# Where the first sets of w1 sums are loaded, and when a tile's results and the w2 sums are made, in a Strassen FFN fused with attention

## The chip, the core and the metric

The kernel runs on one core of one Trainium2 chip. The metric is the time of one execution on the device in microseconds (us), lower is better. Three runs of the kernel before took 535.15, 537.13 and 540.07 us; the median is 537.13 us. A change of about 1% (5.4 us) is what a measurement of this kernel can tell from no change.

## What is computed

```python
scores = scale * np.matmul(q, k.transpose(0, 1, 3, 2))      # q, k, v: 8 x 12 x 448 x 64
x = np.matmul(np.maximum(scores, 0.0) ** 2 / S, v)          # then as tokens: 8 x 448 x 768
mu = np.mean(x, axis=-1, keepdims=True)
var = np.mean((x - mu) ** 2, axis=-1, keepdims=True)
xn = (x - mu) / np.sqrt(var + 1e-06) * g_ln
out = x + np.maximum(xn @ w_ch1, 0.0) @ w_ch2               # w_ch1: 768 x 3072, w_ch2: 3072 x 768
```

There is no softmax: the scores are cut at zero and squared. The 1/sqrt(var) of the layer norm is applied after the second product, as a factor of each token, and g_ln and the mean are folded into w1.

## The kernel before, in words

The eight batches are worked on in four pairs (0 to 3) of 896 tokens. Each pair goes through attention, a first FFN product (xn @ w_ch1, then a relu on ScalarE) and a second one. TensorE's work is interleaved by hand: `interleave` (L13) hands out the attention of pair p+1 in bundles of three score tiles between the units of the second FFN product of pair p. Every engine runs its instructions in program order, so an instruction that waits holds up all that stand behind it on its engine. A bundle is 12 matmuls `sc_ps` (L364), three relus on ScalarE (L375), and squares, two on VectorE (L379) and, for pairs 1 and 3, one on ScalarE (L377).

From pair 1 on, the first FFN product is a Strassen product (`ffn1_pair`, L763). w1 and x are cut in 2 x 2 blocks, and seven products of sums of blocks take the place of eight. Its function `run` (L921) goes through 12 steps (n = 0 to 11); a step has seven products of three matmuls of 448 columns, in the order 3, 4, 1, then 7 and 6 of the step before (`close`, L862), then 5 and 2. Beside them ScalarE copies the first result to `z` (L928) and does the relus (L857), and VectorE does four additions (L930, L932, L944, L947). Products 5 and 2 cannot start before the copy (L928) and the first addition (L930) of their step. Products 1, 2, 5, 6 and 7 take sums of blocks of x (`x_sum`, made at the stage's start by `start`, L880, and by `even` and `odd`, L869 and L876).

The five sums of blocks of w1 that a step needs, a *set*, are computed once, in pair 1's first FFN product, and written to a DRAM tile `kept`. Pairs 2 and 3 load them again (`given`): `sums_early(n)` (L804) loads what products 3, 4 and 1 read, on SyncE's queue for sets 0 to 2 and on ScalarE's for the others; `sums_late(n)` (L820) loads what products 6 and 7 read, on SyncE's queue. There is room for three sets at a time. Set 0 lies in `room0`. For pair 2, sets 1 and 2 lie in four buffers of the pool `attn`, which holds the squared scores (`w_sum` in the profile). For pair 3, the last, all pools of the attention (`heads`, L78) are closed first, and a new pool `late` in their place (`prepare`, L1167) holds the sets (`w_room`) and five sums of x.

SyncE's queue carries, in program order, the writes of the results (`out_dram`, L756, two for each half tile), these loads, the transposing DMAs of k and q for the attention (L311, L316, L317), and the DMAs that transpose x to tokens (`xtok_sb`, L637). For pair 3 these last are 24: six at the hook `odd` (L1195), and three, three, six and six in the steps 0 to 3 (`between_three`, L1187). Eight DMA semaphores are handed out in turn to the DMAs of the two queues, SyncE's and ScalarE's, and a DMA is not issued before the previous one on its semaphore has landed. In the program, ScalarE's load of set 7, which stands between the relus of step 4 and the copy L928 of step 5, shares its semaphore with the first of the six transposes that belong to step 3.

`between_two` (L1171) puts the sums of blocks of w2, which the Strassen form of the second FFN product of pairs 2 and 3 reads, into pair 2's first FFN product: t3 and t4 as 24 subtractions on GpSimd (L988), two a step, and t7 as three additions on VectorE (L985), one in each of the steps 1 to 3. t1 and t6 are made earlier, by six additions on VectorE beside pair 1's second FFN product (L1249), and take two quarters of w1 that no step reads any more; t7 lies in `spare`.

The second FFN product of pairs 2 and 3 is `strassen_units` (L1197). A token tile has 128 tokens, and a pair seven tiles: the odd one, tile 3, is done directly in `ffn2_mid` (L1013), and the other six, as three pairs of tiles, by seven products each (`ffn2_pair`, L1048). `ffn2_mid` accumulates in two PSUM banks, one for each half of the columns; `finish` (L741) computes the result of a half on VectorE (L745), which frees the bank, and stores it. The sums of h that the first pair of tiles needs are made by `h_sums_of` (L999): s1 (L1007), s2 and s5 (L1005), s6 (L1009), s7 (L1011). The first product of `ffn2_pair` takes the first of these two banks for pair 2; for pair 3 it takes other banks.

A few lines that the change touches (L1035 to L1046):

```python
        nc.vector.tensor_add(s[:, n], h[:, 0, n], h[:, 1, n])
        for name in ("s1", "s2", "s6", "s7"):
            h_sums_of(pair, 0, (name,))
        yield from most(a, s, "t2")
        yield
        yield from most(b, s, "t5")
        yield
        ...
        for half, ps in enumerate((a, b)):
            finish(pair, 3, half, 0, K1, ps, (nc.sync, nc.sync))
```

Of the kernel before, what the change touches and what calls it, by code (L numbers as in the profile page):

```python
# [28 lines left out]
def kernel(  # L29
# [733 lines left out]
    def ffn1_pair(pair, keep=False, given=False, prepare=None, between=None):  # L763
# [8 lines left out]
        w, temps, rooms = {}, [], [None] * 3  # L772
        kinds = {3: (0, 3), 4: (3, 6), 1: (6, 9), 6: (9, 12), 7: (12, 15), "16": (6, 12)}

        def room_of(t, late=None):

            if t is None:
                return {}
            r = {m: t[:, a:b] for m, (a, b) in kinds.items() if b <= t.shape[1]}
            if late is not None:  # L780
                r.update({m: late[:, a - 9:b - 9] for m, (a, b) in kinds.items() if a >= 9})
            r["early"] = [(t[:, :9], 0)]
            r["late"] = [(t[:, 9:] if late is None else late, 9)]
            return r
        rooms[0] = room_of(room0)
# [5 lines left out]
        wide_x = prepare is not None  # L791

        def x_sum(m, a, b, op):
            if wide_x:
                op(x[m], a, b)
            else:
                op(x[m][0], a[:, :2], b[:, :2])
                op(x[m][3], a[:, 2], b[:, 2])
# [5 lines left out]
        def sums_early(n):  # L804
# [4 lines left out]
            w[n].update(rooms[n % 3])  # L809
# [10 lines left out]
        def sums_late(n):  # L820
            if n >= KH:
                return
            if given:
                w[n].update(rooms[n % 3])
                fetch(nc.sync, n, "late")
                return
# [42 lines left out]
        def even():  # L869
            sums_early(0)  # L870
            if not wide_x:
                nc.vector.tensor_add(x[5], lo[:, :KQ], lo[:, KQ:])
                sums_late(0)
                sums_last(0)

        def odd():  # L876
            if not wide_x:
                nc.vector.tensor_sub(x[6], hi[:, :KQ], lo[:, :KQ])

        def start():  # L880
            z = x_room[:, 0].rearrange("p c s -> p (c s)")
            temps.extend(z[:, i * S2:(i + 1) * S2].bitcast(fp32) for i in range(2))
            if wide_x:
                pool = prepare()
                for i in range(3):
                    t = pool.tile([P, 6 if i == 0 else 15, P], bf16, tag=f"w1_{i}", name=f"w1_room{i}")
                    rooms[i] = room_of(room0[:, :9], t) if i == 0 else room_of(t)
                xs = pool.tile([P, 5, KQ, S], bf16, tag="x_sum", name="x_sum")
                x.update({m: xs[:, i] for i, m in enumerate((1, 2, 7, 5, 6))})
                sums_late(0)  # L890
            else:
                hold_x = [apool.tile([P, 2, 512], bf16, tag="attn", name="x_sum")[:, :, :S] for _ in range(5)]
                for m, t, rest in ((1, 0, (3, 0)), (2, 1, (3, 1)), (7, 2, (4, 0))):
                    x[m] = (hold_x[t], hold_x[t][:, 0], hold_x[t][:, 1], hold_x[rest[0]][:, rest[1]])
                for i in range(1, 3):
                    one, two = (apool.tile([P, 2, 512], bf16, tag="attn", name="w1_sum")
                                .rearrange("p r (c n) -> p (r c) n", n=P) for _ in range(2))
                    if given:
                        rooms[i] = {3: one[:, :3], 4: one[:, 3:6], 1: (None, one[:, 6], one[:, 7], two[:, 0]),
                                    6: two[:, 1:4], 7: two[:, 4:7],  # L900
                                    "early": [(one, 0)], "late": [(two[:, :7], 8)]}
                    else:
                        rooms[i] = {3: two[:, :3], "4a": one[:, 6:8], "4b": two[:, 6],
                                    4: (None, one[:, 6], one[:, 7], two[:, 6]),
                                    1: one[:, :3], 6: one[:, 3:6], 7: two[:, 3:6], "16": one[:, :6]}
            if given:
                for n in (1, 2):
                    sums_early(n)
                    sums_late(n)
            x_sum(1, lo[:, :KQ], hi[:, KQ:], nc.vector.tensor_add)  # L910
            if wide_x:
                x_sum(5, lo[:, :KQ], lo[:, KQ:], nc.vector.tensor_add)
            x_sum(2, hi[:, :KQ], hi[:, KQ:], nc.vector.tensor_add)
            x_sum(7, lo[:, KQ:], hi[:, KQ:], nc.vector.tensor_sub)
            if wide_x:
                x_sum(6, hi[:, :KQ], lo[:, :KQ], nc.vector.tensor_sub)
# [56 lines left out]
    def w2_sum_units(name):  # L973
# [5 lines left out]
        def four(c):  # L979
            if name == "t7":  # L980
                to = w2_sum[name][:, 4 * c:4 * c + 4]
            else:
                at = w1[:, c, KH * P:] if name == "t1" else w1[:, KQ + c, :KH * P]
                to = at.rearrange("p (k n) -> p k n", n=DH)
            nc.vector.tensor_add(to, x[:, 4 * c:4 * c + 4], y[:, 4 * c:4 * c + 4])  # L985

        def one(k):
            nc.gpsimd.tensor_sub(w2_sum[name][:, k], x[:, k], y[:, k])  # L988
        if name in ("t3", "t4"):
# [23 lines left out]
    def ffn2_mid(pair, a, b):  # L1013
# [22 lines left out]
        for name in ("s1", "s2", "s6", "s7"):  # L1036
            h_sums_of(pair, 0, (name,))
        yield from most(a, s, "t2")
        yield
        yield from most(b, s, "t5")  # L1040
        yield
        for half, ps, left, name, then in ((0, a, h[:, 1], "t4", "t2"), (1, b, h[:, 0], "t3", "t5")):
            rows(ps, left, name, n, KH)
            rows(ps, s, then, n, KH, last=True)
        for half, ps in enumerate((a, b)):
            finish(pair, 3, half, 0, K1, ps, (nc.sync, nc.sync))  # L1046

# [119 lines left out]
    def prepare():  # L1167
# [145 lines left out]
```

## Time and profile before

The profiled execution took 538.45 us, of which its span, from the first to the last instruction, is 536.5 us; the median of the three runs is 1.32 us under it.

| what | value |
|---|---|
| span of the profiled execution | 536.5 us |
| TensorE busy | 514.6 us, 96% of the span |
| VectorE busy | 384.0 us, 72% |
| ScalarE busy | 308.9 us, 58% |
| GpSimd busy | 109.7 us, 20% |
| mean granted TensorE clock | 0.986 |
| pair 2's first FFN product, 297 to 354 us | TensorE busy 53.61 us of 57 |
| its second one, beside pair 3's attention, 354 to 425 us | 66.94 us of 71 |
| pair 3's first FFN product, 425 to 491 us | 59.26 us of 66 |
| its second one, 491 to 536.5 us | 41.26 us of 45.5 |

How to read it: in a row of instructions, *engine line operation out<-in* is followed by the count; in the timeline the first two columns are the start and the duration in us, and a bracket tells the idle time of the engine before the row and what ended it. "SPq" and "ACTq" are DMA issues on the queues of SyncE and ScalarE. A list of waits gives the sum in us, the count and the longest. A row of a window gives busy time of each engine, the granted clock as a share of the full one, the share of time in which the DMA engines were busy, and GB/s.

### The profile page before, as it was taken

To read this page: it belongs to the slowest core of one execution; us is meant where nothing else is said; L and a number is where in the kernel's file an instruction comes from. 1 tells how busy PE (TensorE), PEld (TensorE's weight loads), DVE (VectorE), ACT (ScalarE), POOL (GpSimd) and SP (SyncE) were. 2 spreads that over 40 slices of the span, in tenths; PEclk is the share of its full clock that TensorE was granted. 3 is DMA by queue.
4 is the path that set the end of the run, shared out by engine and by line. 5 is a ranking of instruction groups with operands and counts; after the bars stand their busy time and mean duration, and the time that the engine had idled before them with its cause. 6 is when DMAs were issued, how large, how long until landed. Compare 5 with 4: busy or idle time off the path is not lost.

```text
span 536.5 us, 11444 instructions
## 1 busy us (share of the span) xinstructions
PE 514.6 (96%) x4565; PEld 302.4 (56%) x4565; DVE 384.0 (72%) x723; ACT 308.9 (58%) x495; POOL 109.7 (20%) x150
## 2 busy tenths in 40 slices
PE   8999999999999999999999899989999977999996
PEld 6687779755555545555555445544555434455663
DVE  5875754598998998768876598765876836776653
ACT  6966775588584567566463366766878244571000
POOL 7334102112212475002102592001200000000000
PEclk9999999999999999999999899998999989899999
DMA  9999999999899856249959954107983284511222
GB/s 197 206 205 208 211 190 160 149 182 184 150 189 177 171 171 172 67 89 154 156 131 167 224 145 130 55 1 135 165 133 77 51 221 108 152 51 28 62 59 59
DMA packets 125478, 74.34 MB, mean 139 GB/s; under 512 B 80882, under 2 KB 121842, under 8 KB 125426
## 3 DMA queue, kind: packets, MB, share of 16 engines
q1 hardware_dynamic: 94994, 42.17, 39.6%
q0 software_dynamic: 26976, 25.50, 31.4%
q10 hardware_dynamic: 3456, 5.97, 3.9%
q8 instruction: 35, 0.57, 0.5%
q14 instruction: 17, 0.14, 0.1%
HBM read 63.70 MB, written 16.91 MB: 150 GB/s over the span
## 4 chain that ended last, share of the span: by engine, by line
PE 88%; DVE 3%; ACT 3%; DMA 2%; SPq 2%; issue 2%; ACTq 0%
PE m_ps L853 26%; PE o_ps L734 19%; PE m_ps L1064 8%; PE h_ps L675 7%; PE o_ps L1064 7%; PE sc_ps L364 7%; PE av_ps L396 6%; PE o_ps L1023 2%; PE h_ps L719 2%; PE h_ps L701 2%; ACT early L375 1%; DMA w_sum<-kept 1%; ACT attn_sb L375 1%; PE tr_ps L249 1%; PE idle_ps L235 1%
## 5 line engine op out<-in xcount | busy, mean ns | idle before, releaser
L375 ACT ACTIVATE attn_sb<-sc_ps 128x896 bf16<-128x896 f32 (+4 forms) x150 | 126.2, 902 | 51.6 <-PE sc_ps L364 43.7
L734 PE MATMUL o_ps<-w,hT_sb 128*128 128x384 bf16 x672 | 116.0, 326 | 0.0
L857 ACT ACTIVATE hT_sb<-m_ps 128x448 bf16<-128x448 f32 x144 | 78.1, 544 | 56.3 <-PE m_ps L853 53.7
L734 PEld LDWEIGHTS <-hT_sb 128*128 128x128 bf16 x672 | 63.0, 98 | 48.8 <-issue 10.1
L379 DVE TENSOR_TENSOR attn_sb<-attn_sb 128x896 bf16<-128x896 bf16 x98 | 59.8, 621 | 32.8 <-ACT attn_sb L375 32.2
L675 PE MATMUL h_ps<-x_room,w 128*128 128x256 bf16 (+2 forms) x384 | 43.8, 263 | 0.3 <-ACT early L375 0.3
L928 ACT COPY x_room<-m_ps 128x448 f32<-128x448 f32 x36 | 19.1, 532 | 37.0 <-PE m_ps L853 31.4
L1064 PEld LDWEIGHTS <-hT_sb 128*128 128x128 bf16 x288 | 27.8, 98 | 20.1 <-issue 2.5
L944 DVE TENSOR_TENSOR m_ps<-x_room,m_ps 128x448 f32<-128x448 f32 x36 | 22.6, 628 | 22.9 <-ACT hT_sb L857 22.5
L675 PEld LDWEIGHTS <-w 128*128 128x128 bf16 x384 | 33.8, 97 | 7.0 <-issue 2.6
L853 PE MATMUL m_ps<-x_sum,w 128*128 128x448 bf16 x144 | 33.3, 352 | 4.4 <-ACT x_room L928 2.8
L853 PEld LDWEIGHTS <-w_sum 128*128 128x128 bf16 x240 | 23.4, 98 | 24.6 <-DMA w_sum<-kept 2.4
L853 PEld LDWEIGHTS <-w 128*128 128x128 bf16 x216 | 21.1, 98 | 25.2 <-issue 5.7
L402 DVE TENSOR_SCALAR xT_sb<-av_ps 128x896 bf16<-128x896 f32 (+2 forms) x30 | 27.0, 900 | 10.6 <-PE av_ps L396 10.4
L158 POOL DMA_DIRECT2D k_sb<-in_k_dram x15 | 10.7, 712 | 107.6 <-DMA kT_sb<-k_sb 83.9
L1064 PEld LDWEIGHTS <-x_room 128*128 128x128 bf16 x216 | 20.9, 99 | 19.3 <-issue 6.4
L158 POOL DMA_DIRECT2D v_sb<-in_v_dram x20 | 14.2, 711 | 83.1 <-PE sc_ps L364 74.5
L364 PE MATMUL sc_ps<-qT_sb,kT_sb 64*64 64x448 bf16 x392 | 28.5, 364 | 1.2 <-ACT hT_sb L857 0.6
L930 DVE TENSOR_TENSOR x_room<-x_room,m_ps 128x448 f32<-128x448 f32 x36 | 21.6, 600 | 10.0 <-ACT x_room L928 5.9
L652 DVE BATCH_NORM_STATS2 stats<-xtok_sb 128x6 f32<-128x384 bf16 x56 | 28.3, 547 | 0.1
L685 ACT ACTIVATE hT_sb<-h_ps 128x256 bf16<-128x256 f32 (+1 forms) x49 | 18.0, 368 | 16.0 <-PE h_ps L675 15.1
L377 ACT ACTIVATE attn_sb<-attn_sb 128x896 bf16<-128x896 bf16 x28 | 26.6, 950 | 0.9
(170 smaller groups left out, 846.8 us busy)
## 6 DMA issues: line engine op xcount, KB each, us to landing
out_dram<-o_room SPq DMA_DIRECT2D x108, 96.0 KB, 2.2
w<-in_moe_w_ch_dram POOLq DMA_DIRECT2D x12, 384.0 KB, 14.2
w<-in_moe_w_ch_dram POOLq DMA_DIRECT2D x4, 1152.0 KB, 20.5
q_sb<-in_q_dram POOLq DMA_DIRECT2D x20, 224.0 KB, 5.9
v_sb<-in_v_dram POOLq DMA_DIRECT2D x20, 224.0 KB, 6.0
k_sb<-in_k_dram POOLq DMA_DIRECT2D x15, 224.0 KB, 5.9
w_room<-kept SPq DMA_DIRECT2D x12, 192.0 KB, 2.7
kept<-room SPq DMA_DIRECT2D x4, 480.0 KB, 2.8
```

The costliest lines, as they stand in the source:

```text
L364: nc.tensor.matmul(ps[cols, r, o * w:(o + 1) * w], g["k"](i)[rows, cols], g["q"](i, r)[rows, blk[0]:sum(blk), cols], start=True, stop=True)
L375: nc.scalar.activation(a, ps[:, :, :len(slots) * w], ACTF.Relu)
L377: nc.scalar.activation(a, a, ACTF.Square)
L379: nc.vector.tensor_mul(a, a, a)
L396: nc.tensor.matmul(ps[cols, hh, :w], v_sb[rows, pr, j * D:(j + 1) * D], g["attn"][i][rows, r, :], start=(j == 0), stop=(j == J - 1))
L402: nc.vector.tensor_scalar_mul(x, ps[:, :, :w], score_scale)
L652: nc.vector.bn_stats(stats[:, n], xtok[pair][:, n * G:(n + 1) * G, t, :])
L675: nc.tensor.matmul(ps[:, :w + more], w1[:, c, ni * P:(ni + 1) * P], xc[b][:, c, s.start:s.stop + more], start=(c == 0), stop=(c == K1 - 1))
L734: nc.tensor.matmul(ps[:, :DH], hT[pair][:, ki, t * P:(t + 1) * P], w2[:, ki, cols], start=(o == 0), stop=(o == K2 - 1))
L853: nc.tensor.matmul(ps, *at, start=(first and c == 0), stop=(c == KQ - 1), skip_group_check=not first)
L857: nc.scalar.activation(hT[pair][:, n + KH * row, half * S:(half + 1) * S], ps, ACTF.Relu)
L1064: nc.tensor.matmul(ps, x[:, ki], y[ki] if isinstance(y, list) else y[:, ki], start=(first and ki == 0), stop=(ki == KH - 1), skip_group_ch ...
```

## The change

- **Pair 2's sets 1 and 2** are loaded at the hook `even`, behind set 0, into the quarter of w1 that t1 took until then, instead of into `w_sum` at the stage's start. Set 4 and later go to the `attn` buffers as before.
- **Pair 3's sets.** The pools of the attention are no longer closed, and there is no pool `late`. The rest of set 0 and the sets 1 and 2 are loaded at the hook `odd`, ahead of the six token transposes, into the buffers of q and k, whose last transposes are done. The sums x5 and x6 are made at `odd` too, in the two buffers of transposed q; the other three x sums take `attn` buffers in six additions, as in pairs 1 and 2.
- **`ffn2_mid`** finishes the first half tile before it starts the second one's last products, and puts each half's result ahead of the sums of h: s1, result, s2 with s5, result, s6, s7. It is one unit shorter, three units in place of four are kept for after the attention, and no bundle is placed ahead of the units.
- **w2 sums.** t1 moves from VectorE, beside pair 1's second FFN product, to GpSimd in pair 2's first one: 12 additions behind the 24 subtractions, three a step. t7 moves from the steps 1 to 3 of that stage to VectorE beside pair 1's second FFN product. t6 stays there at other units.

The matmuls are the same in number and shape. The diff, cut to its core:

```diff
-    def ffn1_pair(pair, keep=False, given=False, prepare=None, between=None):
+    def ffn1_pair(pair, keep=False, given=False, late=False, between=None):
...
+        def room_of_two(one, two):
+            return {3: one[:, :3], 4: one[:, 3:6], 1: (None, one[:, 6], one[:, 7], two[:, 0]),
+                    6: two[:, 1:4], 7: two[:, 4:7], "early": [(one, 0)], "late": [(two, 8)]}
...
+        rooms[0] = room_of(room0, room0[:, 9:])
+        if late:
+            rooms[0] = room_of(room0[:, :9], chunks(slots["k"][1], 6))
+            rooms[1] = room_of_two(chunks(qbuf[0], 8), chunks(qbuf[1], 7))
+            rooms[2] = room_of_two(chunks(qbuf[2], 8), chunks(slots["k"][0], 7))
+            for m, t in ((5, slots["qT"][1]), (6, slots["qT"][0])):
+                x[m] = t.rearrange("p a b -> p (a b)")[:, :KQ * S].rearrange("p (c s) -> p c s", s=S)
+        elif given:
+            quarter = [chunks(w1[:, c, KH * P:], KH) for c in range(KQ)]
+            for n in (1, 2):
+                once[n] = room_of(quarter[n - 1][:, :9], quarter[2][:, 6 * (n - 1):6 * n])
...
-            w[n].update(rooms[n % 3])
+            w[n].update(once.get(n) or rooms[n % 3])
...
         def even():
             sums_early(0)
-            if not wide_x:
+            if not late:
                 nc.vector.tensor_add(x[5], lo[:, :KQ], lo[:, KQ:])
                 sums_late(0)
                 sums_last(0)
+                if given:
+                    for n in (1, 2):
+                        sums_early(n)
+                        sums_late(n)
 
         def odd():
-            if not wide_x:
-                nc.vector.tensor_sub(x[6], hi[:, :KQ], lo[:, :KQ])
+            if late:
+                nc.vector.tensor_add(x[5], lo[:, :KQ], lo[:, KQ:])
+                for n in range(3):
+                    if n:
+                        sums_early(n)
+                    sums_late(n)
+            nc.vector.tensor_sub(x[6], hi[:, :KQ], lo[:, :KQ])
...
-            if given:
-                for n in (1, 2):
-                    sums_early(n)
-                    sums_late(n)
...
         def one(k):
-            nc.gpsimd.tensor_sub(w2_sum[name][:, k], x[:, k], y[:, k])
-        if name in ("t3", "t4"):
+            if name == "t1":
+                nc.gpsimd.tensor_add(w2_sum[name][k], x[:, k], y[:, k])
+            else:
+                nc.gpsimd.tensor_sub(w2_sum[name][:, k], x[:, k], y[:, k])
+        if name in ("t3", "t4", "t1"):
...
-        for name in ("s1", "s2", "s6", "s7"):
-            h_sums_of(pair, 0, (name,))
-        yield from most(a, s, "t2")
-        yield
-        yield from most(b, s, "t5")
-        yield
+        h_sums_of(pair, 0, ("s1",))
         for half, ps, left, name, then in ((0, a, h[:, 1], "t4", "t2"), (1, b, h[:, 0], "t3", "t5")):
+            if half:
+                yield
+            yield from most(ps, s, then)
             rows(ps, left, name, n, KH)
             rows(ps, s, then, n, KH, last=True)
-        for half, ps in enumerate((a, b)):
             finish(pair, 3, half, 0, K1, ps, (nc.sync, nc.sync))
+            for more in (("s2",), ("s6", "s7"))[half]:
+                h_sums_of(pair, 0, (more,))
...
-            side.update(gps=w2_sum_units("t3") + w2_sum_units("t4"), t7=w2_sum_units("t7"),
+            side.update(gps=w2_sum_units("t3") + w2_sum_units("t4") + w2_sum_units("t1"),
                         tokens=token_units(2, range(NT)))
...
-        if 0 < n <= KQ:
-            side["t7"].pop(0)()
-        for _ in range(2):
+        for _ in range(3):
             side["gps"].pop(0)()
...
-            sums = w2_sum_units("t1") + w2_sum_units("t6")
-            units = beside_of(units, {8 + 6 * n: f for n, f in enumerate(sums)})
+            sums = w2_sum_units("t6") + w2_sum_units("t7")
+            units = beside_of(units, dict(zip((12, 20, 28, 43, 45, 47), sums)))
...
-        few = 4 if last else 3
-        interleave(units[:-few], beside, 0, 1 if last else 0)
+        few = 3
+        interleave(units[:-few], beside)
         for f in left:
             f()
         wide.close()
-        if last:
-            heads.close()
         hook("start")
```

## The prediction

> **What bounds the kernel now.** The page gives TensorE 96% of the span, so only its idle time and its slow clock can be gained; no work on it is added or removed. I read the list of TensorE's waits first, because it tells how long it stood still and for whom.
>
> ```profile
> PE m_ps L853 <- DMA w_room<-kept: 3.5, 1, 3.5
> PE o_ps L1064 <- DVE o_room L745: 3.2, 1, 3.2
> PE m_ps L853 <- ACT x_room L928: 2.8, 1, 2.8
> PE m_ps L853 <- DMA w_sum<-kept: 2.0, 1, 2.0
> PE m_ps L853 <- DVE x_room L930: 1.6, 2, 1.1
> ```
>
> These five are 13.1 us. By the timeline they lie, in order: A, 300.11 to 302.08, pair 2's step 1 waits for set 1, which SyncE issued only at 295.76; B, 319.28 to 320.43, step 4 waits for VectorE; C, 360.25 to 363.41, the first product of `ffn2_pair`; D, 428.62 to 432.11, pair 3's step 1 waits for set 1 (with 0.47 for VectorE just ahead of it); E, 452.70 to 455.48, pair 3's step 5 waits for ScalarE's copy L928.
>
> Second, windows behind these places, for the granted clock (busy times of PE, PEld, DVE, ACT and POOL, then the clock, the DMA share and GB/s).
>
> ```profile
> 300.00:305.00 5.00, 3.03 (x12) 1.36 (x12) 2.21 (x5) 1.20 (x3) 3.52 (x5) 0.81 1.16 314
> 305.00:310.00 5.00, 5.00 (x23) 2.37 (x22) 2.33 (x4) 2.71 (x5) 5.00 (x7) 0.84 1.21 141
> 364.00:368.00 4.00, 4.00 (x24) 1.57 (x22) 1.42 (x3) 2.92 (x4) 0.00 (x0) 0.57 0.66 143
> 432.00:436.00 4.00, 3.89 (x13) 1.72 (x14) 1.24 (x2) 0.53 (x1) 0.00 (x0) 0.61 0.97 284
> 456.00:482.00 26.00, 26.00 (x130) 12.97 (x128) 20.40 (x42) 16.72 (x33) 0.00 (x0) 0.93 0.36 105
> ```
>
> A, C, D and E are each followed by lost clock: 5 x 0.19 + 5 x 0.16 = 1.75 us, 4 x 0.43 = 1.72, 4 x 0.39 = 1.56, 26 x 0.07 = 1.82. I take 1.7 us for each: a stall that goes takes this with it. B, of 1.15 us, has no such stretch behind it.
>
> Third, the timelines of C and E, and SyncE's queue ahead of E.
>
> ```profile
> 357.28 0.95 DVE L1007 TENSOR_TENSOR x_room<-hT_sb 128x1536 bf16<-128x1536 bf16 x1
> 358.15 1.75 DVE L1005 TENSOR_TENSOR x_room<-hT_sb 128x3072 bf16<-128x3072 bf16 x1
> 359.93 0.96 DVE L1009 TENSOR_TENSOR hT_sb<-hT_sb 128x1536 bf16<-128x1536 bf16 x1
> 360.81 0.95 DVE L1011 TENSOR_TENSOR hT_sb<-hT_sb 128x1536 bf16<-128x1536 bf16 x1
> 362.75 1.13 DVE L745 SCALAR_TENSOR_TENSOR o_room<-o_ps,rstd_sb,xtok_sb 128x384 f32<-128x384 f32 x2
> 363.41 0.81 PE L1064 MATMUL o_ps<-w,x_room 128*128 128x384 bf16 x4 [3.15 <-DVE o_room L745]
> ```
>
> At C the matmuls of the odd tile are done at 360.25; its result, which frees the bank, stands on VectorE behind all the sums of h and two squares.
>
> ```profile
> 418.43 1.11 SPq L756 DMA_DIRECT2D out_dram<-o_room  x2
> 419.58 7.70 SPq L637 DMA_TRANSPOSE xtok_sb<-xT_sb  x6
> 427.39 1.17 SPq L756 DMA_DIRECT2D out_dram<-o_room  x2
> 428.79 2.31 SPq L789 DMA_DIRECT2D w_room<-kept  x5
> ...
> 452.20 7.47 SPq L637 DMA_TRANSPOSE xtok_sb<-xT_sb  x6
> ```
>
> ```profile
> 454.47 0.33 ACTq L789 DMA_DIRECT2D w_room<-kept  x1
> 454.89 0.53 ACT L928 COPY x_room<-m_ps 128x448 f32<-128x448 f32 x1 [4.45 <-DMA xtok_sb<-xT_sb]
> 455.48 1.38 PE L853 MATMUL m_ps<-x_sum,w 128*128 128x448 bf16 x6 [2.78 <-ACT x_room L928]
> ```
>
> E is not what its name says: ScalarE stood 4.45 us at its load of set 7, whose semaphore waits for the first transposing DMA issued at 452.20; that landed at 454.45. SyncE issues one such transpose in 7.70 / 6 = 1.28 us and was busy with them almost without a break from 434.20 to 459.67.
>
> **The change part by part**, as differences to the profiled execution, 538.45 us, which is 1.32 us above the median of the runs.
>
> *Pair 2's sets 1 and 2 at `even`.* The loads move some 25 us ahead of their old place at 295.76. A goes, with its stretch: -1.97 - 1.7 = -3.7 us. What could be late next is the load of set 3 or the step-3 transposes; the latter land about 310.1, and ScalarE's copy behind them is needed about 310.9, so there is 0.8 us of cover. On SyncE the four loads, 0.57 us each, go in front of six token transposes, six stores and 36 transposes of k and q; they push these 2.3 us. SyncE stands idle for TensorE's results ahead of 286.88, which swallows it, and the store's buffers are three deep: 0, and at most +2.3 if that idle time is used up.
>
> *t7 and t1.* B goes: -1.15. VectorE's three L985 there took 1.25, 1.47 and 1.69 us; without them a step of it is 2.5 us and 1.2 of layer-norm statistics, under the step's 4 us or so. Beside pair 1's second product VectorE has three additions of t1 less and three of t7 more, 0.94 us each: 0. GpSimd gets 12 additions: its group L988 has 24 in 23.1 us, 0.96 to 1.0 each. From 301.6 on, 36 of them end by 338 at the earliest, or with step 11 about 349 as they are handed out; the first product reads t1 at about 354. Cost 0, covered by 5 to 16 us.
>
> *`ffn2_mid` of pair 2.* In C, only s1 (0.95 us) remains ahead of the first result, and s2 with s5 (1.75) ahead of the second. From the rows, the first result is done at about 356, s2 at 358.3, the second at 360; TensorE, which has one score bundle less to do first, comes to the product at about 358.9 and finds its bank free. The wait of 0.63 us for ScalarE at 353.73, which stood before that bundle (`sc_ps` behind `hT_sb`), goes too: -3.15 - 0.63 - 1.7 = -5.5. Bounds: -3.0, if one wait of 0.8 us comes back and the slow stretch stays, and -5.9, if another 0.4 is saved on squares. One bundle more must find room later in the product: 17 of them in 43 units, three of ScalarE's relus (2.54 us) each, 43 us of some 70; not binding.
>
> *Pair 3's sets at `odd`.* D goes as a stall: -3.5 - 1.7 = -5.2 if nothing else were there, -5.7 with the 0.47 ahead of it. But E is set by SyncE, not by TensorE. Count SyncE's issues from the store at 418.43 to the first transpose of step 3 at 452.20, 33.8 us before. The change puts the five loads first, and every instruction stays: at 1.29 us a transpose, 0.57 a store and 0.46 to 0.57 a load: 2 stores 1.15, 5 loads 2.4, 6 transposes 7.74, 6 stores 3.45, 3 transposes 3.87, load 0.57, 3 transposes 3.87, load 0.57, 6 transposes 7.74, load 0.57; sum 31.9. Only 1.8 us of waiting is saved. The copy L928 and TensorE follow as before: 455.48 - 1.8 = 453.6. TensorE comes there 5.2 us earlier, at 447.5, so E grows from 2.8 to about 6.2 us and its slow stretch stays. D and E together: -1.8. Bounds: 0 (SyncE gains nothing) and -5.7 (SyncE moves with TensorE). I take -1.8, since the queue's count is the nearest row. The x sums of `start` in six additions rather than five, and x5 and x6 at `odd`, lie on VectorE where the first step waited 0.47 us for it: 0, between -0.47 and +0.5.
>
> *The last `ffn2_mid`* (pair 3) uses other banks and has no stall over 0.25 us: 0.
>
> Sum: -3.7 - 1.15 - 5.5 - 1.8 = -12.2, to 526.3 us for such an execution, **525.0 us** for the median. The ends of the bounds are -1.97 - 1.15 - 3.0 - 0 = -6.1 (531.0) and -3.7 - 1.15 - 5.9 - 5.7 = -16.5 (520.7).
>
> The Trainium skill, page "TensorE: Matmul & The Clock Gate", section "Why this matters for your kernels", says to have "No PE-idle gaps >~3µs between matmul bursts", as a window of idle puts the clock back to half. By that rule A's 1.97 us and E's 2.78 would cost no clock, and the sum would be 1.7 less for A, 526.7 us. Here the trace disagrees with it: 0.81 and 0.84 of the clock stand behind 1.97 us of idling.
>
> **Rivals.**
> *R1, SyncE moves with TensorE.* E stays 2.8 us, D's gain of 5.2 is whole. For it: the queue also waited, at 428.56 and 433.60. Against it: those waits are 0.8 us in all, and the transposes stand back to back. 538.45 - 3.7 - 1.15 - 5.5 - 5.2 - 1.32 = 521.6 us.
> *R2, the transposes also hold pair 2.* Its load of set 5 stands on ScalarE behind its third step-3 transpose in the same way as E; the cover is 0.8 us, and TensorE now comes 3.7 us earlier. If they land 2 us too late against it, 2.2 + 1.7 = 3.9 us are given back: 528.9; with C's gain at its lower end, 531.4, and more than that if both are worse. For it: at 299.75 four transposes took 5.32 us. Against: SyncE no longer has the four loads of 2.59 us in front of them.
> *R3, GpSimd is too slow: slower.* The first product of `ffn2_pair` needs t1, and through it all 36 GpSimd additions, between 301.6 and 354. From 52.4 / 36 = 1.46 us each TensorE waits there, and from (52.4 + 12.2) / 36 = 1.79 us each the change loses: at 1.9 us each they end at 370, 16 late: 538.45 - 12.2 + 16 - 1.32 = 540.9. For it: VectorE's L985 went from 0.94 alone to 1.69 beside GpSimd. Against: GpSimd's own rows stayed at 0.96 to 1.0 there.
> *R4, the stalls go but come back elsewhere in full*, as E does with D: about 536. For it: E. Against: A and C have no saturated queue behind them.
> *R5, the clock needs longer idling than A's*: 526.7, as worked out from A's 1.7 us; against it stand the two rows named. This is the rule quoted above.
>
> **How the numbers follow.** Forecast 0.56, R1 0.12, R2 0.20, R3 0.03, R4 0.05, R5 0.04. The forecast's own range is 523 to 528 (the phase of the slow stretches, 1.7 us either way, and C's bounds). R1 reaches down to 521, R2 up to 531.8 with 0.06 of its 0.20 above. Left outside 521.0 to 531.8 are that 0.06, R3, R4 and some 0.03 below: 0.17. About 1%, 5.4 us, is what a measurement of this kernel can tell from no change. Faster by more, under 531.8: 0.56 + 0.12 + 0.14 + 0.04 = 0.86. Within 1%: 0.06 + 0.05 = 0.11. Slower: 0.03.
>
> **What would show it.** In the waits of TensorE of the changed kernel there is none for a DMA from `kept` (A, D), none of 1 us for L930 in pair 2 (B), none for L745 ahead of the first product of `ffn2_pair` (C), and one of about 6 us for the copy L928 in pair 3's step 5, with ScalarE's load issued right after the landing of a transpose (E grown). Two stretches of half clock less remain. The group L988 has 36 additions of about 1 us. The forecast is wrong if E stays under 3 us (R1), if a wait for L928 appears in pair 2's steps 3 to 5 (R2), or if TensorE waits for L988 (R3).

## The result, and the profile after

The changed kernel takes 530.18 us (median of 7 runs, 527.09 to 532.75); the kernel before took 536.57 us in the same comparison (7 runs, 533.91 to 540.07). The ratio is 0.988, with a 95% interval of 0.984 to 0.992: 6.4 us faster, where 12.2 were forecast. The profiled execution took 529.36 us (span 527.6), 9.1 us less than the profiled one before. The difference between 6.4 and 9.1 is itself a finding: the profiled execution of before was 1.9 us above its median, for a reason that is shown below. In one of the experiments, the third, three of ten runs fell into a slower state; its ratio leaves them out, its median does not.

By stages (from the first start of a matmul `m_ps` of a first FFN product to the last one's, from there to the next stage, and for pair 3 to the end of the span):

| profiled execution | pair 2, first product | pair 2, second product | pair 3 | span |
|---|---|---|---|---|
| before | 56.27 | 71.61 | 111.51 | 536.50 |
| changed | 53.18 | 66.64 | 110.50 | 527.59 |
| difference | -3.09 | -4.97 | -1.01 | -8.91 |
| forecast | -4.85 | -5.5 | -1.8 | -12.2 |

TensorE's list of waits of the changed kernel, in us (sum, times, longest):

```profile
PE m_ps L863 <- DMA q_sb<-kept: 4.8, 2, 4.3
PE m_ps L863 <- DMA k_sb<-kept: 2.3, 1, 2.3
PE m_ps L863 <- ACT x_room L928: 1.8, 1, 1.8
PE idle_ps L235 <- DVE ones L97: 1.1, 1, 1.1
PE sc_ps L364 <- DVE xT_sb L402: 0.9, 1, 0.9
```

The five old waits are gone; the one name that stays, the copy L928, now stands in pair 2 instead of pair 3, and two waits for `kept` are new. The 1.8 us lie in pair 2, at 307.08, a step after the place of A. The timeline there:

```profile
298.86 0.72 POOL L158 DMA_DIRECT2D v_sb<-in_v_dram  x1
300.32 6.82 SPq L637 DMA_TRANSPOSE xtok_sb<-xT_sb  x4
307.83 0.36 ACTq L805 DMA_DIRECT2D w_sum<-kept  x1
308.29 0.53 ACT L928 COPY x_room<-m_ps 128x448 f32<-128x448 f32 x1 [3.47 <-DMA xtok_sb<-xT_sb]
308.87 0.73 PE L863 MATMUL m_ps<-x_room,w 128*128 128x448 bf16 x3 [1.79 <-ACT x_room L928]
```

ScalarE is stopped at its load (307.83, set 4) until the first of the four transposes has landed, at 307.81, 7.5 us after its issue. It lies among the three loads of k, q and v that GpSimd issued from 297.44 on; the last of them took 8.1 us to land. This is the mechanism of E, met in pair 2, at step 2.

The 4.3 and 2.3 us lie in pair 3, in steps 4 and 5:

```profile
431.43 3.80 SPq L637 DMA_TRANSPOSE xtok_sb<-xT_sb  x3
433.25 0.54 PE L863 MATMUL m_ps<-x_sum,q_sb 128*128 128x448 bf16 x2
435.33 0.52 SPq L805 DMA_DIRECT2D q_sb<-kept  x1
435.90 7.50 SPq L637 DMA_TRANSPOSE xtok_sb<-xT_sb  x6
438.13 0.36 PE L863 MATMUL m_ps<-x_sum,q_sb 128*128 128x448 bf16 x1 [4.34 <-DMA q_sb<-kept]
443.50 0.52 SPq L805 DMA_DIRECT2D k_sb<-kept  x1
446.29 0.36 PE L863 MATMUL m_ps<-x_sum,k_sb 128*128 128x448 bf16 x1 [2.33 <-DMA k_sb<-kept]
446.46 0.33 ACTq L805 DMA_DIRECT2D q_sb<-kept  x1
446.88 0.53 ACT L928 COPY x_room<-m_ps 128x448 f32<-128x448 f32 x1 [3.86 <-PE m_ps L863]
447.62 0.73 PE L863 MATMUL m_ps<-qT_sb,w 128*128 128x448 bf16 x3
```

Product 1 has done two of its three matmuls and stops for the third. In the new rooms (`room_of_two`) the third block of product 1 comes with the *late* load, on SyncE's queue behind the transposes; in the pool `late` it came with the early one, on ScalarE's. So SyncE holds this stage as forecast (4.3 + 2.3 = 6.6 us, forecast 6.2), but directly, by two loads, not through ScalarE. ScalarE's load of set 7, issued at 446.46, is 0.2 us behind, so the forecast's own wait stood ready at the same place. The last row is product 5 of step 5, the point at which E ended before.

At C (L1009 now makes s1, L1007 s2 and s5) the results stand where the diff puts them, and the product meets a free bank, 5.2 us after the stage's start where it was 10.0:

```profile
351.55 0.95 DVE L1009 TENSOR_TENSOR x_room<-hT_sb 128x1536 bf16<-128x1536 bf16 x1
352.94 0.62 DVE L745 SCALAR_TENSOR_TENSOR o_room<-o_ps,rstd_sb,xtok_sb 128x384 f32<-128x384 f32 x1 [0.45 <-PE o_ps L1025]
353.47 1.75 DVE L1007 TENSOR_TENSOR x_room<-hT_sb 128x3072 bf16<-128x3072 bf16 x1
355.65 2.11 PE L1065 MATMUL o_ps<-w,x_room 128*128 128x384 bf16 x12
```

Windows for the clock (columns as in the prediction; a *slow stretch* is a time in which about half the clock is granted):

```profile
307.00:311.00 4.00, 2.21 (x12) 1.07 (x11) 1.94 (x4) 2.58 (x6) 4.00 (x6) 1.00 1.18 247
438.00:442.00 4.00, 3.87 (x12) 1.63 (x13) 0.62 (x1) 1.24 (x3) 0.00 (x0) 0.57 0.12 25
442.00:446.00 4.00, 1.96 (x11) 0.79 (x9) 2.39 (x5) 0.93 (x2) 0.00 (x0) 1.00 0.31 82
446.00:450.00 4.00, 3.71 (x20) 1.97 (x21) 2.28 (x4) 2.65 (x6) 0.00 (x0) 1.00 0.38 90
```

Only the stall of 4.34 us is followed by a slow stretch (4 x 0.43 = 1.7 us). Those of 1.79 and 2.33 us are not. So three of the four stretches are gone, at 1.7 us each 5.1 us of the 9.1.

### The profile page after: what moved, and what is told of

Its sections match the earlier page's. It is cut to its first block, busy times and chain, and to the rows that moved or that the text cites. A ratio compares the mean times of both kernels' runs of the same rounds, so it can differ in the third digit from the quotient of the medians.

```text
span 527.6 us, 11443 instructions
## 1 busy us (share of the span) xinstructions
PE 508.7 (96%) x4565; PEld 300.2 (57%) x4565; DVE 380.2 (72%) x723; ACT 308.7 (59%) x495; POOL 117.9 (22%) x162
## 4 chain that ended last, share of the span: by engine, by line
PE 85%; DMA 5%; DVE 3%; ACT 2%; SPq 1%; issue 1%; POOL 1%; ACTq 0%; DVEq 0%; POOLq 0%
PE m_ps L863 24%; PE o_ps L734 20%; PE m_ps L1065 8%; PE h_ps L675 7%; PE sc_ps L364 6%; PE av_ps L396 6%; PE o_ps L1065 6%; PE o_ps L1025 3%; PE h_ps L719 2%; PE h_ps L701 2%; DMA v_sb<-in_v_dram 2%; DMA xtok_sb<-xT_sb 1%; DMA q_sb<-kept 1%; ACT early L375 1%; ACT attn_sb L375 1%
## 5 line engine op out<-in xcount | busy, mean ns | idle before, releaser
L928 ACT COPY x_room<-m_ps 128x448 f32<-128x448 f32 x36 | 19.1, 531 | 34.1 <-PE m_ps L863 28.6
L863 PEld LDWEIGHTS <-w 128*128 128x128 bf16 x246 | 24.2, 98 | 25.8 <-issue 3.9
L675 PEld LDWEIGHTS <-w 128*128 128x128 bf16 x384 | 33.8, 97 | 7.2 <-issue 2.8
L402 DVE TENSOR_SCALAR xT_sb<-av_ps 128x896 bf16<-128x896 f32 (+2 forms) x30 | 27.0, 900 | 9.9 <-PE av_ps L396 9.8
L863 PEld LDWEIGHTS <-w_sum 128*128 128x128 bf16 x210 | 20.4, 98 | 19.5 <-POOL w_sum L826 0.5
L863 PE MATMUL m_ps<-x_sum,w 128*128 128x448 bf16 x120 | 29.2, 353 | 0.1
L932 DVE TENSOR_TENSOR x_room<-x_room,m_ps 128x448 f32<-128x448 f32 x36 | 22.4, 621 | 7.0 <-PE m_ps L863 3.4
L930 DVE TENSOR_TENSOR x_room<-x_room,m_ps 128x448 f32<-128x448 f32 x36 | 21.6, 599 | 7.9 <-ACT x_room L928 7.9
```

The lines of the kernel that those rows point to most:

```text
L402: nc.vector.tensor_scalar_mul(x, ps[:, :, :w], score_scale)
L675: nc.tensor.matmul(ps[:, :w + more], w1[:, c, ni * P:(ni + 1) * P], xc[b][:, c, s.start:s.stop + more], start=(c == 0), stop=(c == K1 - 1))
L863: nc.tensor.matmul(ps, *at, start=(first and c == 0), stop=(c == KQ - 1), skip_group_check=not first)
```

## The experiments

The theory: the waits were taken away as planned, but the DMA queues put others in place of A and D, since transposes on SyncE's queue hold ScalarE (by shared semaphores) and the late loads (by their order). The rivals: the new layout of the sets costs the time; buffers come free too late; or the earlier loads were worth little.

**1. `ffn2_mid` alone**, on the kernel before: the new body of `ffn2_mid`, its count of units and the interleaving that goes with it, nothing else of the change.

```diff
-        for name in ("s1", "s2", "s6", "s7"):
-            h_sums_of(pair, 0, (name,))
...
+        h_sums_of(pair, 0, ("s1",))
...
-        few = 4 if last else 3
-        interleave(units[:-few], beside, 0, 1 if last else 0)
+        few = 3
+        interleave(units[:-few], beside)
```

> The kernel before with the new ffn2_mid alone. If the waits of C are what this part removes and nothing takes their place, pair 2's second product shrinks from 71.6 us to about 66.6 as in the changed kernel (-5.0, of which 1.7 is clock), and the whole by 5 us, to 0.991 of before. Rival: C's gain needs the earlier t1 or the other order of sums as well; then the stage stays above 69 us. All other waits of before (A, B, D, E) stay within 0.5 us.

Measured: 530.05 us, 0.992 of before (0.989 to 0.995). Pair 2's second product takes 67.13 us, 4.5 less. So C, without any other part, brings 0.8% where the whole change brings 1.2%, and the two intervals overlap. And one wait of before is missing from the top of the list, although nothing was done about it:

```profile
PE m_ps L853 <- DMA w_room<-kept: 2.7, 1, 2.7
PE m_ps L853 <- ACT x_room L928: 2.6, 1, 2.6
PE m_ps L853 <- DVE x_room L930: 2.4, 2, 1.4
```

A is down to 0.31 us, and pair 2's first product takes 52.79 us with the same instructions that took 56.27. SyncE issued the load of set 1 at 294.75, not at 295.76, and it landed at 300.43, not at 302.03. The expectation that A stays was wrong. The two waits of D changed shape too, though not in sum: 1.4 us for VectorE and 2.7 for the load, 0.5 and 3.5 before.

**2. The kernel before once more**, for a second profile (no edit).

> The kernel before once more, for a second profile. Theory that A is an accident of one execution (the loads of set 1 land among GpSimd's loads of q, k and v, so that 1 us decides): no wait for set 1 at pair 2's step 1, or a shorter one, and pair 2's first FFN product takes about 52.8 us as in the run with ffn2_mid alone, not 56.3; span about 533. Rival, that A belongs to the kernel and the other run was the accident: the wait of 2.0 us and 56.3 us again.

Measured: span 533.4 us, and

```profile
PE m_ps L853 <- DMA w_room<-kept: 4.0, 1, 4.0
PE o_ps L1064 <- DVE o_room L745: 3.2, 1, 3.2
PE m_ps L853 <- ACT x_room L928: 2.1, 1, 2.1
PE m_ps L853 <- DMA w_sum<-kept: 1.8, 1, 1.8
```

Neither theory has it whole: A is back, with 1.8 us, but no slow stretch follows it, and the stage takes 53.74 us. B was 0.41 us here. So A with its stretch is worth 3.7 us in one of three executions of these instructions, 1.8 in another and 0.3 in the third. The other stages differ as well. Pair 2's second product takes 72.79 us, 1.2 more than in the first profile, with two slow stretches at C in place of one (360.11 to 366.93). Pair 3 takes 109.67, 1.8 less, with no slow stretch behind E.

**3. Pair 3's sets as before**, the rest of the change kept: the changed kernel with the old `prepare`, pool `late` and five x sums.

```diff
-    def ffn1_pair(pair, keep=False, given=False, late=False, between=None):
+    def ffn1_pair(pair, keep=False, given=False, prepare=None, between=None):
...
+                pool = prepare()
+                for i in range(3):
+                    t = pool.tile([P, 6 if i == 0 else 15, P], bf16, tag=f"w1_{i}", name=f"w1_room{i}")
...
+        if last:
+            heads.close()
```

> The changed kernel, but pair 3's sets as before: pools closed, pool late, loads at start. Theory that SyncE's queue holds pair 3's stage: the stage has its old waits (3.5 us for a load at step 1, 2.8 us for ScalarE's copy at step 5) in place of the new ones (4.3 and 2.3 us for kept), and from its first matmul to the end of the span it takes 111.5 us against 110.5 in the changed kernel; the whole 1 us slower than the changed kernel. Rival, that moving the loads earlier bought the whole 5 us of D: 4 to 5 us slower than the changed kernel.

Measured: 532.87 us (0.994 of before, 0.990 to 0.997). Pair 3 takes 111.31 us, 0.8 more than in the changed kernel, with

```profile
PE m_ps L857 <- ACT x_room L936: 4.9, 2, 3.0
PE m_ps L857 <- DMA w_room<-kept: 2.6, 1, 2.6
PE m_ps L857 <- DVE x_room L938: 1.4, 1, 1.4
```

This is the 1 us that the theory has for loading pair 3's sets earlier. But both profiles are single executions, the two of before differ by 1.8 us in this stage, and the times do not settle it either: the ratios 0.994 and 0.988 differ by 0.6%, with intervals that overlap. And the wait for ScalarE in pair 2 is in this kernel too (1.89 us at 307; the first row adds it to E's 3.0), so it belongs to pair 2's part. Against experiment 1, pair 2's first product is not shorter at all (53.28 and 52.79 us).

**4. Product 1's third block with the early part**, on ScalarE's queue.

```diff
-                    6: two[:, 1:4], 7: two[:, 4:7], "early": [(one, 0)], "late": [(two, 8)]}
+                    6: two[:, 1:4], 7: two[:, 4:7], "early": [(one, 0), (two[:, :1], 8)], "late": [(two[:, 1:7], 9)]}
```

> The changed kernel with the last block of product 1 loaded with the early part, on ScalarE's queue, not with the late part on SyncE's. Theory that SyncE's transposes hold the stage whichever way: the waits of 4.3 and 2.3 us for kept go, but ScalarE's load of a set then waits for a transpose of step 3 and TensorE waits about 5 to 6 us for the copy L928; pair 3's part stays at 110.5, within 1 us. Rival, that the layout alone costs: no such wait, and 6 to 8 us less (6.7 us of waits and 1.7 of clock).

Measured: 534.05 us (0.996 to 1.002 of before), pair 3 113.06 us, 2.6 worse than the changed kernel. The waits for `kept` are gone, and in their place stands

```profile
PE m_ps L863 <- ACT x_room L928: 9.2, 5, 3.7
```

One of the five, 1.85 us, is pair 2's; the other 7.4 us are pair 3's. The theory's wait came, larger and in more places than its 5 to 6 us, and the stage did not stay at 110.5: for two of every three sets ScalarE now has two loads in place of one that can share a semaphore with a transpose. That this is why it is larger was not tried. The rival, that the layout alone costs, falls.

**5. Fewer transposes at once.**

```diff
-        if n < 4:
-            tokens_part(3, *((3, 6, range(3)), (3, 6, range(3, K1)), (2, 3, range(K1)), (6, 7, range(K1)))[n])
+        if n < 2:
+            tokens_part(3, 3, 6, range(3 * n, 3 * n + 3))
+        elif n < 8:
+            t, c = (2, 2 * n - 4) if n < 5 else (6, 2 * n - 10)
+            tokens_part(3, t, t + 1, range(c, c + 2))
```

> The changed kernel with the token transposes of tiles 2 and 6 of pair 3 issued two a step in steps 2 to 7, not six in step 2 and six in step 3. Theory that the queue of transposes holds the stage: the wait of 2.3 us goes, the one of 4.3 us stays or shrinks a little, since the six transposes of steps 0 and 1 are still ahead of that load; from 110.5 to about 107 us. Rival, that the loads are late for another reason (buffers, DMA bandwidth): both waits stay, 110.5.

Measured: 526.43 us (0.979 to 0.991 of before); pair 3 takes 106.21 us, 4.3 less than in the changed kernel. The waits for `kept` are gone; one stall of 3.44 us is left, for ScalarE, which waits 5.11 us behind a late load of SyncE's:

```profile
433.48 0.53 SPq L805 DMA_DIRECT2D k_sb<-kept  x1
434.05 3.80 SPq L637 DMA_TRANSPOSE xtok_sb<-xT_sb  x3
436.17 0.33 ACTq L805 DMA_DIRECT2D q_sb<-kept  x1
436.59 0.53 ACT L928 COPY x_room<-m_ps 128x448 f32<-128x448 f32 x1 [5.11 <-DMA k_sb<-kept]
437.17 1.28 PE L863 MATMUL m_ps<-qT_sb,w 128*128 128x448 bf16 x3 [3.44 <-ACT x_room L928]
```

So the number of transposes ahead of the loads decides; with buffers that come free too late both waits would have stayed. Pair 2's wait for ScalarE was 3.18 us in this run, with a slow stretch behind it (56.16 us for the stage): that stage varies as much after the change as before it.

**6. Pair 2's transposes a step later.**

```diff
-    soon = {(1, "even"): (0, 3, range(K1)), (1, "run"): (3, NT, range(2)), (2, "odd"): (0, 2, range(K1))}
+    soon = {(1, "even"): (0, 3, range(K1)), (2, "odd"): (0, 2, range(K1))}
...
-        if n < 2:
-            tokens_part(2, 3, NT, range(2 * n + 2, 2 * n + 4))
-        elif n > 2 and side["tokens"]:
+        if 0 < n < 4:
+            tokens_part(2, 3, NT, range(2 * n - 2, 2 * n))
+        if n > 2 and side["tokens"]:
```

> The changed kernel with pair 2's token transposes of tiles 3 to 6 two a step in steps 1 to 3, not two ahead of step 0, two in step 0 and two in step 1. Theory that the wait of 1.8 us for the copy L928 at 307 is ScalarE held by the landing of the first of these transposes, which lie among GpSimd's loads: the wait goes and pair 2's first FFN product takes 51.0 to 51.5 us in place of 53.2. Rival, that DMA traffic of that moment holds ScalarE's load whatever stands ahead of it: a wait of over 1 us stays, or moves one step on, 53 us.

Measured: 527.71 us (0.983 to 0.993 of before; the profiled executions here and in experiment 7 reach pair 1's first product at 178.6 us, the others at 175.1 to 175.6, so stages and not spans are compared). Pair 2's first product takes 51.14 us, without a wait of over 0.4 us in it; the waits that are left on top are pair 3's:

```profile
PE m_ps L863 <- DMA q_sb<-kept: 4.6, 2, 4.2
PE m_ps L863 <- DMA k_sb<-kept: 1.9, 1, 1.9
```

The wait for ScalarE was the landing of these transposes. This is what A and B are worth once nothing takes their place: 1.7 us against experiment 1, 2.6 against the second profile of before, 5.1 against the first.

**7. Pair 3's sets on GpSimd's queue.**

```diff
-                fetch(nc.scalar if n > 2 else nc.sync, n, "early")
+                fetch((nc.gpsimd if late else nc.scalar) if n > 2 else nc.sync, n, "early")
...
-                fetch(nc.sync, n, "late")
+                fetch(nc.gpsimd if late and n > 2 else nc.sync, n, "late")
```

> The changed kernel with sets 3 to 11 of pair 3 loaded on GpSimd's queue, which has no other work then, the transposes where they are. Theory that in pair 3 the loads are late only because they stand behind transposes in a queue or behind them on a shared semaphore: no wait for kept or for the copy L928 of over 0.5 us, pair 3's part 110.5 - 6.7 - 1.7 = 102.1 us (to 103.5 with a little left). Rival, that buffers come free too late or the DMA engines are too busy: waits of 3 us or more stay, over 107 us.

Measured: 523.18 us, 0.978 of before (0.969 to 0.986). Pair 3 takes 101.21 us, 9.3 less than in the changed kernel, and the longest wait is now pair 2's:

```profile
PE m_ps L863 <- ACT x_room L928: 2.1, 1, 2.1
```

The transposes are where they were; the loads only no longer stand behind them or share their semaphores. Buffers and DMA bandwidth held nothing. Which of the two, the order in a queue or the shared semaphore, costs how much this run does not tell apart.

**8. t7 back on VectorE in pair 2's steps 1 to 3.**

```diff
-                        tokens=token_units(2, range(NT)))
+                        t7=w2_sum_units("t7"),
+                        tokens=token_units(2, range(NT)))
...
+        if 0 < n <= KQ:
+            side["t7"].pop(0)()
...
-            sums = w2_sum_units("t6") + w2_sum_units("t7")
+            sums = w2_sum_units("t6")
```

> The changed kernel with the three additions of t7 back on VectorE in pair 2's steps 1 to 3. If B is theirs: a wait of 0.5 to 1.2 us for L930 in steps 3 to 4 of pair 2, and its first FFN product takes 53.2 to 54.4 us. Rival, that the wait of 1.8 us for ScalarE in step 2 has given VectorE time to catch up: no such wait, 53.2.

Measured: B is back, with 0.67 us (0.41 and 1.15 in the two profiles of before):

```profile
317.54 1.21 DVE L984 TENSOR_TENSOR spare<-w 128x1536 bf16<-128x1536 bf16 x1
318.67 1.01 DVE L652 BATCH_NORM_STATS2 stats<-xtok_sb 128x6 f32<-128x384 bf16 x2
319.84 0.57 DVE L930 TENSOR_TENSOR x_room<-x_room,m_ps 128x448 f32<-128x448 f32 x1
320.47 0.73 PE L863 MATMUL m_ps<-x_sum,w 128*128 128x448 bf16 x3 [0.67 <-DVE x_room L930]
```

The stage took 56.25 us, more than expected: the wait for ScalarE was 2.35 us and had a slow stretch behind it. One execution, so the time of 533.3 us says little.

**9. What D is worth with a free queue**: experiment 3 with pair 3's sets 3 to 11 on GpSimd's queue (the edit of 7, with `wide_x` for `late`).

> The changed kernel with pair 3's sets 0 to 2 loaded as before (pools closed, pool late, loads at start) and sets 3 to 11 on GpSimd's queue. Theory that D was worth what the prediction's term says, once SyncE's transposes hold nothing: the wait for set 1 stays (1.4 + 2.6 us and a slow stretch of 1.7 in most executions), E goes, so pair 3's part is 101.2 + 4.0 to 5.7 = 105 to 107 us, against 111.3 with ScalarE's and SyncE's queues. Rival, that the free queue alone makes the difference: about 101 to 103.

Measured: 529.13 us (0.982 to 0.993 of before); pair 3 takes 109.89 us, 8.7 more than with sets 0 to 2 loaded early (experiment 7). The longest waits are these; the first and the third stand at the start of pair 3, the second is pair 2's:

```profile
PE m_ps L857 <- DMA w_room<-kept: 5.1, 1, 5.1
PE m_ps L857 <- ACT x_room L936: 2.1, 1, 2.1
PE m_ps L857 <- DVE x_room L938: 1.4, 1, 1.4
```

The theory holds, and the size is above its 4.0 to 5.7: the wait for set 1 is 5.1 us, not 2.6, and two slow stretches lie at it (426.31 to 433.13). Set 1 took 5.36 us to land, 2.89 in experiment 3; GpSimd's load of set 3 was issued ahead of it here, at 421.33, and on ScalarE's queue only at 424.53, after set 1 had landed. Whether that explains all of the 2.5 us was not tried. The same edit is worth 0.8 us with one queue and 8.7 with another, by one profile each (101.2 us twice on the faster side, in experiments 7 and 11). By the ratios of all runs, 0.988 and 0.978, the second is 1.0%, 5.3 us, again with intervals that overlap.

**10. The changed kernel once more** (no edit).

> The changed kernel once more, for a second profile: pair 2's first FFN product 53 to 56 us with a wait of 1.8 to 3.2 us for the copy L928 at about 307, pair 2's second product 66.6, pair 3's part 110.5 with waits of 4 and 2 us for kept. Whether a slow stretch follows a wait should go by where the wait lies in the clock's windows, not by its length alone.

Measured: span 526.9 us; pair 2 53.47 and 66.43 us, pair 3 109.96, with waits of 2.08, 3.84 and 2.60 us at the old places, of which only the one of 3.84 has a slow stretch behind it. These two profiles of the changed kernel agree within 0.6 us in every stage, though experiments 5, 8 and 9 show that a stretch can follow pair 2's wait as well. The first profile of before was a long execution of its kernel: its span of 536.5 us is above all 38 of before in the later comparisons (527.9 to 535.1).

**11. Both queue edits together** (6 and 7) on the changed kernel.

> The two edits that took waits away, together: pair 3's sets 3 to 11 on GpSimd's queue, pair 2's token transposes two a step in steps 1 to 3. The waits lie in different stages, so the gains should add: pair 2's first FFN product 51.1 us, pair 3's part 101.2, no wait of TensorE over 1 us after the first 20 us, span about 520, time about 0.972 of before and below both kernels. Rival, that the later transposes or the earlier finish of pair 2 bring a new wait: 2 us or more of it given back.

Measured: 518.57 us against 535.33, a ratio of 0.971 (0.967 to 0.975): faster than both kernels. The stages are 51.14, 67.09 and 101.20 us, so the gains add. What TensorE still waits for, beside the start:

```profile
PE sc_ps L364 <- DVE xT_sb L402: 1.2, 2, 0.9
PE sc_ps L364 <- ACT attn_sb L375: 0.9, 1, 0.9
```

## Why the prediction was right or wrong, step by step

The direction was right, and about half of the size. 530.18 us lies above the forecast's own range of 523 to 528 and inside the range as a whole, because that reaches up to 531.8 for R2, the rival whose mechanism came true.

- **A, -3.7: the step that failed.** The wait for set 1 went. But the prediction took a cover of 0.8 us ahead of the step-3 transposes as enough, and looked at the wrong step: the *first* transposes held ScalarE at step 2, and TensorE for 1.79 to 3.18 us, in all eight profiles with sets 1 and 2 loaded at `even` and pair 2's transposes left in place. Its rival R2, at 0.20, described this for a later load (set 5, steps 3 to 5), with 2.2 us and a stretch; the mechanism came in each of the eight, earlier than R2 said, with a stretch in three. The term behind it is one that was put at 0: the 2.3 us by which the four loads push SyncE's transposes of k and q were to be swallowed by idle time ahead of 286.88. The transpose that was issued at 286.88 before is issued at 288.68 in the changed kernel, and GpSimd's loads of k, q and v, which wait for a transpose of k, come 3.8 us later. Their first row before, then in the changed kernel:

```profile
293.64 0.72 POOL L158 DMA_DIRECT2D k_sb<-in_k_dram  x1 [8.46 <-DMA kT_sb<-k_sb]
297.44 0.71 POOL L158 DMA_DIRECT2D k_sb<-in_k_dram  x1 [7.73 <-DMA kT_sb<-k_sb]
```

In the three profiles with the old loads (both of before and experiment 1) they begin 3.5 to 4.7 us ahead of the stage, and the first token transpose lands 5.0 to 5.3 us after its issue. In the eight they begin between 3.1 us ahead and 0.7 behind the stage's start, and it lands after 7.2 to 9.3 us. That the later loads slow it is read from these rows, not tried by itself, and in experiment 4, where they begin 3.1 us ahead, it takes 7.2 us already. And the 3.7 us were those of one execution: in three executions of the same instructions A and its stretch cost 3.7, 1.8 and 0.3. So A brought about nothing on balance (experiments 1 and 3), where 3.7 was forecast.
- **B, -1.15: right in mechanism.** It is 0.4 to 1.15 us by execution, and 0.67 when t7 is put back alone.
- **t1 on GpSimd, 0: right.** 24 and 12 additions of 0.90 us each end at 333, far from the first product at 355.65. R3 needed 1.46. The row of the 12:

```profile
L988 POOL TENSOR_TENSOR w<-w 128x384 bf16<-128x384 bf16 x12 | 10.5, 900 | 0.0
```

- **C, -5.5: right.** -4.97 against the first profile of before, -4.48 alone, and -6.36 between the two second profiles, where before has two stretches here. The wait, the 0.63 ahead of it and the stretch went. What came back is 0.94 us in which the scores wait for VectorE's L402; another 0.45 is for a transposing DMA of q, where the same stage of before had 0.55 for ScalarE. The bounds (-3.0 to -5.9) held the -4.97.
- **D and E, -1.8: the queue is the reason, as forecast (experiments 5, 7 and 9), but the saving was mis-sized, and the -1.0 is luck.** The count of SyncE's issues said 31.9 us from the store to the first step-3 transpose; it was 33.5 (410.53 to 444.07), 1.1 of the 1.6 more because one transpose of step 0 took 2.41 in place of 1.29. Before it was 33.8, so the queue saved 0.2 us, not 1.8. TensorE shows the same: product 5 of step 5 starts 30.5 us after the stage's start before (455.48) and 30.5 after it in the changed kernel (447.62). In the four profiles with pair 3's old loads (both of before, experiments 1 and 3) it is 30.3 to 30.5 us, in the four with the new ones (both of the changed kernel, experiments 6 and 8) 30.0 to 30.7. What is 1.0 us shorter comes behind this point, where the first profile of before has E's slow stretch; the second has none there, and takes 109.67 us, less than either profile of the changed kernel. The stretch of the changed kernel (438.41 to 441.82) lies ahead of this point, between two waits for the queue, so the second wait takes it up. The named wait was wrong too: not the copy L928 but two loads for `kept`, because the prediction did not see that `room_of_two` moves product 1's third block from the early load to the late one, and so makes the late one due a step earlier.
- **The clock.** There are three stretches fewer, as the sum had it (A, C, D); the one that is left stands behind the 4.34 us, not at E. The last part of the prediction wrote two, which did not agree with its own sum.
- **The basis.** The sum was made against an execution with four stretches and A whole. Second profiles (5.1 us of lost clock and A at 1.8 in before) show that part of what was counted as the change's gain was that execution's share of bad luck. Between the two second profiles the span is 6.5 us shorter, near the 6.4 of the medians, and by stages it is -0.3, -6.4 and +0.3 us: there C is the whole gain.

Nothing here tests R5's threshold by itself, but the runs speak to it. The Trainium skill, page "TensorE: Matmul & The Clock Gate", Part 1, describes the gate by windows of idling of about 3.4 us. Here stretches are 3.41 us long or twice that, and within one execution they all start at the same phase of windows of 3.41 us; idle times of 1.97 us (before) and 2.15 (experiment 9) had one behind them and 2.33 (changed) and 2.60 (experiment 10) had none. So the length alone, by which R5 goes, does not decide.

## What to carry to other kernels

Before a stall is counted as a gain, follow each queue that the engine behind it depends on, and ask where the next load or transpose of that queue will stand when the engine comes earlier: here taking D away was worth 0.8 us behind a queue full of transposes and 8.7 beside a free one, by one profile each. Where a DMA is issued by a computing engine, look at which DMA had its semaphore before; that engine stands still until the other has landed (3.47 us of ScalarE's time in pair 2). And take two profiles before a sum: a wait that hangs on 1 us of DMA timing, with its slow clock, can be 3.7 us in one execution and 0.3 in another.

## What the runs showed of the hardware

- Whether an idle time costs clock goes by where it lies, not by its length alone. If windows of 3.41 us are laid by the stretches of the same profile, the 1.97 us of A fill 58% of one window and have a stretch, as have 2.15 us in one window (experiment 9, 63%); the 2.60 us of experiment 10 lie with 1.84 in one window (54%) and the rest in the one before, and have none. That the limit is between 54 and 58% of a window is read from these, not tried by itself. It holds for a window at the full clock. A window that was slow itself was followed by another slow one when it was idle for 26, 31, 40, 63 and 74% (experiments 2, 8, 4, 6 and 9), and by the full clock when it was idle for 21% or less (20 windows; those at the end of a span, where the work ends, are left out).
- A transpose of the tokens lands 2.4 us after its issue in pair 3 of the changed kernel (the one of 444.07, DMA share 0.3 to 0.4), and 7.5 us after (9.3 in experiment 5) beside GpSimd's loads of q, k and v in pair 2 (the one of 300.32, DMA share 1.2 from 307 to 311).
- VectorE's three additions of t7 cost GpSimd time too: the 24 rows L988 of before have a mean of 997 ns (a median of 907 and a longest of 1630), the same 24 of the changed kernel, without t7 beside them, 901, and with t7 put back (experiment 8) 997 again.
